# Three chained layers on one core: first-stage tiles shifted by 32 bytes, a bit step moved from GpSimd to VectorE, and stores, spools, weight loads and second-MLP inputs given other slots and places

## The chip, the cores and the metric

The kernel runs on one core of a Trainium2 chip. The metric is the device time of one execution in microseconds (us). The engines are TensorE (PE; its weight loads are PEld), VectorE (DVE), ScalarE (ACT), GpSimd (POOL) and SyncE (SP). Each works through its own queue in program order. SP issues every DMA of this kernel, so a DMA that must wait holds all DMAs behind it.

## The reference

```python
scores = scale * np.matmul(q_c, k_c.transpose(0, 1, 2, 4, 3))    # chunks of 64 positions
attn = softmax(scores); out = np.matmul(attn, v_c)               # 8 x 8 heads, 576 x 64 -> x: 4608 x 512
gate = 1.0 / (1.0 + np.exp(-(x @ w_gate)))                       # 512 x 1536
x = (gate * (x @ w_val)) @ w_out                                 # 1536 x 512
h = x @ w_in                                                     # 512 x 2048
g = np.where(h >= 1, h, np.where(h <= -1, 0.0, (h + 1) ** 2 / 4))
return g @ w_out2                                                # 2048 x 512
```

The activations arrive as float32, the weights as 64-bit floats, which the kernel must turn into float32 itself.

## The kernel before

**Precision.** Every large product is done as three fp32r matmuls of a high and a low part (`three`, L455 to L457). A weight tile goes through a chain of steps: `w_load` (DMA of the 64-bit words into a tile called raw), `w_low` (L114, a multiply and a min on the lower words), `w_bits` (L120 on DVE, L124 on ACT), `w_join` (L128, DVE), then the split into high (ACT) and low (POOL) parts.

**Stage 1** (0 to 795 us) goes over nine blocks of 512 rows. A block has 24 slots, and a slot is one projection: 12 matmuls of 512 columns, gate and value by turns. Between the projections of block b lies the chunk attention of block b+1 for four pairs of heads, by the methods of `Whole`: transpose, scores (S), maximum and subtraction on DVE, exponential on ACT, sum and reciprocal on DVE (L337 to L340), the scaling on POOL (`w`, L345, tile sp), a transpose of the result on PE (PT, L351), and the product with V (O). The gate times the value is formed on DVE (L854, tile sg) and stored to DRAM (gT).

What is issued in which slot is written by hand: `at(slot, prio, fn)` puts a call in a slot, and `emit(slot)` issues the calls ahead of the slot's projection, by the fraction of the slot and then by prio. Block 0 also converts 24 gate and value tiles, most of them one a slot. From slot 26 (block 1) to block 7 the weights of the later layers are prepared in 22 pairs, one in 7 slots, by the table `s_prep`: load, convert, four sums on POOL (L150 to L153), four splits (L172, L173) into tiles called st, and seven DMAs that store (spool) them to DRAM.

**Stages 2 to 4** are the three further products, each with one level of a seven-product block scheme (PO = 1, 5, 6, 2, 7, 3, 4): "o" (x @ w_out, `down`), "i" (h = x @ w_in, `up`) and "p" (g @ w_out2, `down`). Each goes over six groups of 768 rows, in steps of six matmuls of 384 columns (`on(step, prio, fn)` is the table of calls here). A group is 42 steps in "o" and 56 in "i" and "p". Operands are prepared some steps ahead: a subtraction (`op_sub`, L488), the high part (`op_hi`, ACT L492) and the low part (`op_lo`, L499, POOL or DVE). Results are gathered in tiles R; "o" stores them to yT, "i" stores its activations (tile ua) to uT. The weights of a stage come back from DRAM into 28 places of the pool wp (`s_load`, L187), while the stage before still runs.

**Places.** wp lies at the bottom of SBUF; its tiles of 4 KiB start 1,152 bytes above a multiple of 4 KiB. From the top downwards lie a pad of 128 bytes, a larger pad, then the tiles x of stage 1 (4 KiB each, 1,120 bytes above a multiple of 4 KiB), sg and raw. In "o" the operands (tile op) take the places of x.

Of the kernel before, what the change touches and what calls it, by code (L numbers as in the profile page):

```python
# [8 lines left out]
F32 = mybir.dt.float32  # L9
# [20 lines left out]
def kernel(  # L30
# [15 lines left out]
    nc = tc.nc  # L46
    P = 128
# [63 lines left out]

    def w_low(key):
        word = words(raws[key])
        nc.gpsimd.tensor_scalar(  # L114
            out=word(0, I32), in0=word(0, U32), scalar1=2.0**-29, scalar2=7.0, op0=ALU.mult, op1=ALU.min
        )

# [76 lines left out]
    def s_prep(kind, k):  # L194

        half_ = (F1 if kind == "o" else F2) // 2
        a, b = (kind, k), (kind, k + half_)
        return [
            (0, w_load, a), (0, w_load, b), (2, w_low, a), (2, w_low, b), (3, w_bits, a), (4, w_bits, b),
            (5, w_join, a), (5, w_join, b), (6, s_sums, kind, k), (7, s_split, kind, k, 0), (7, s_split, kind, k, 1),  # L200
            (8, s_split, kind, k, 2), (8, s_spool, kind, k, 0), (8, s_spool, kind, k, 1),
            (9, s_split, kind, k, 3), (9, s_spool, kind, k, 2), (10, s_spool, kind, k, 3),
        ]


# [170 lines left out]
    def first_block():  # L376
        ft = ps.tile([P, BS], F32, tag="b5", name="fill")

        def fill(n):
            for _ in range(n):  # L380
                nc.tensor.matmul(ft, lhsT=z[:, :P], rhs=z, start=True, stop=True)

        pieces = []
        for i in range(NW + 1):
            pieces.append((w_bits, keys[i]))
            pieces.append((w_low, keys[i + 1]))
            if i:
                pieces.append((w_split, keys[i - 1]))
        pieces.insert(0, (w_low, keys[0]))
        nl = [0]  # L390

        def wl(n):
            for _ in range(n):
                w_load(keys[nl[0]])
                nl[0] += 1

        def conv(n):
            while n and pieces:
                fn, key = pieces.pop(0)
                fn(key)  # L400
                if fn is w_split and nl[0] < NW + 5:
                    wl(1)
                n -= fn is not w_low
            if pieces and pieces[0][0] is w_low:
                w_low(pieces.pop(0)[1])

        z = pool["sg"].tile([P, BS], F32R, tag="sg", name="z", bufs=4)
        nc.vector.memset(f32(z), 0.0)
        kv_["ident"] = cp.tile([P, P], F32, name="ident")
        make_identity(nc, kv_["ident"])  # L410
        a = Whole(
            0, [["b0", "b2", "b4"], "b1", "b3", "b6", "b7", "b5"],
            lambda nm: wp.tile([P, 2, BS], F32, tag="w", name=nm), "MVMT",
        )
# [115 lines left out]
    def down(kind, nk, tile_, load0, load1, done, first=0):  # L530

        t0, half_ = len(steps), nk * 7
        for g in range(NG):
            for i, (p, k) in enumerate((p, k) for p in PO for k in range(nk)):
# [19 lines left out]
                for m in range(2):  # L554
                    if k == (nk // 2 - 1 if split and m == 0 else nk - 1):
                        dt = m if p != 4 else 0
                        on(t + 1 + dt, 1, down_result, g, p, m)
                        done(t + 1 + dt, g, m, p)

    def down_step(kind, g, p, ks, ms=(0, 1)):  # L560
        for k in ks if isinstance(ks, list) else [ks]:
            o = OP[kind, g, p, k]
            w = s_weight(kind, p, k)
            for m in ms:
                cols = slice(m * P, (m + 1) * P)
                product(p, m, [(k == 0, (w[:, 0, cols], w[:, 1, cols], o[:, 0], o[:, 1]))], g % 2)

    def down_result(g, p, m):
        if p == 1:
            R_[m] = pool["r"].tile([P, 4, N], F32, tag="R", name="R", bufs=3)  # L570
        r = R_[m]
        result(p, banks[BANK[p], m], lambda i: r[:, i])

# [27 lines left out]
    NY = 22  # L601

    def z_tile(i, dt=F32R):
        return pool["za" if i < 14 or i >= NY else "zb"].tile([P, 2, N], dt, tag=f"z{i}", name="z")

    def z_flat(i):
        return z_tile(i, F32).rearrange("p h t -> p (h t)")
# [21 lines left out]
    def up_result(p, m):  # L629
        b = banks[BANK[p], m]  # L630
        if p in (1, 5):
            shape = [P, 2, N] if p == 1 else [P, N]
            R_[p, m] = pool["r"].tile(shape, F32, tag=f"R{p}", name="R", bufs=3 if p == 1 else 4)
        if p == 4:
            nc.scalar.activation(U[1, m][:, 0], b, AF.Relu, scale=0.5, bias=half)
            R_["b", m] = b
        else:
            result(p, b, lambda i: R_[5, m] if i == 3 else R_[1, m][:, i])
# [108 lines left out]
    for i, key in enumerate(keys):  # L747
        if i >= NW + 5:
            at(i - NW - 5, 2.5, w_load, key)
        if i > NW + 1:  # L750
            at(i - NW - 2, 6, w_low, key)
        if i > NW:
            at(i - NW - 1, 6, w_bits, key)
        if i >= NW:
            at(i - NW, 5.5, w_split, key)
# [29 lines left out]
    for i in range(7):  # L785
        on(2 * 7 * F1 // 2 + 6 * i, 9, s_load, "i", i)
    for s in range(1, 7 * F1 // 2, 2):
        on(last + s, 9, s_load, "i", 7 + s // 2)
    on(tc_ - 6, 9, close_pool, "m3")
    on(tc_ - 6, 9.1, open_pool, "za", "za")  # L790
    for i in range(2):
        on(tc_ - 6, 9.2, y_in, 0, i)
    on(tc_, 2, close_pool, "r")
    on(tc_, 2, close_pool, "x")
    on(tc_, 2, close_pool, "pad4")
# [7 lines left out]
    td = len(steps)  # L803
    last = td - 14 * NJ
    for i in range(NWT["p"]):
        on(last + 2 * i + 4, 9, s_load, "p", i)
    for i in range(F2 // 2):
        on(last + 12 + 2 * i, 9, p_in, 0, 0, i)
        on(last + 30 + i if i < 4 else td + i - 4, 9, p_in, 1, 0, i)
# [16 lines left out]
    with tc.manual_schedule():  # L826
# [3 lines left out]
        nc.vector.memset(minus, -0.5)  # L830

        open_pool("pad", "pad", "right")
        pool["pad"].tile([P, 32], F32, name="pad")

        open_pool("pad4", "pad4", "right")
        pool["pad4"].tile([P, 704], F32, name="pad4")
# [8 lines left out]
        for b in range(NB):  # L845
            for f in range(F1):
                slot = NS * b + 2 * f
                emit(slot)
                go = proj(("g", f), b, f"b{f % 2}")
                sg = pool["sg"].tile([P, BS], F32, tag="sg", name="sg", bufs=4)  # L850
                nc.scalar.activation(sg, go, AF.Sigmoid)  # L851
                emit(slot + 1)
                vo = proj(("v", f), b, f"b{2 + f % 2}")
                nc.vector.tensor_tensor(out=sg, in0=vo, in1=sg, op=ALU.mult)  # L854
                nc.sync.dma_start(out=gT[b][f * P:(f + 1) * P, :], in_=sg)
        close_pool("sg")
        assert not ev, ev
        open_pool("r", "rb", "right")
# [2 lines left out]
            fn(*args)  # L861
        for t in sorted(sched):
            run_step(t)
        for key in ("r", "zb", "pad", "za"):
            close_pool(key)


# [28 lines left out]
```

## Time and profile before

| | |
|---|---|
| three timed runs | 1786.47, 1787.66, 1787.59 us (median 1787.59) |
| the profiled execution | 1787.38 us; its span 1785.6 us |
| PE busy | 1699.8 us, 95% |
| PEld, DVE, ACT, POOL busy | 86%, 64%, 48%, 56% |
| mean granted TensorE clock | 0.981 |
| DMA, read and written | 179.83 MB and 125.30 MB, 171 GB/s |

The span runs from the first to the last instruction. The granted clock is 1.0 at 2.4 GHz and 0.5 at 1.2 GHz. A busy PE is not PE at its peak, since matmuls are pipelined; how many matmuls of one kind a stretch holds says more than its busy time.

### The profile page before, as it was taken

The numbers are of one execution on the slowest core, as the hardware profiler recorded it, in microseconds if no ns is written. First come the engines' busy times: TensorE is split into PE (matmuls) and PEld (weight loads), VectorE is DVE, ScalarE is ACT, GpSimd is POOL, SyncE is SP. The second block draws the span as 40 slices with busy tenths as digits, with TensorE's granted clock in tenths as the row PEclk, the third lists the DMA queues.
The fourth block names the chain that finished last, engine by engine and source line by source line (L and its number), as shares of the span: only waits on it lengthen the run. The fifth ranks groups of instructions, "written<-read, shape, count | busy, mean of one in ns | idle before, by whom it ended". The sixth has DMA issues, their size and how long they took to land.

```text
span 1785.6 us, 29925 instructions
## 1 busy us (share of the span) xinstructions
PE 1699.8 (95%) x10658; PEld 1542.2 (86%) x10658; DVE 1147.0 (64%) x1659; ACT 864.8 (48%) x1560; POOL 993.6 (56%) x826
## 2 busy tenths in 40 slices
PE   6889999899899899999999989999999989999998
PEld 5667777677677677889999989999999989999998
DVE  4664444444444453129877757878887798889886
ACT  4553454444444454125555545555555445455553
POOL 4982554565554554017777755434442167777775
PEclk8899999999999999999999999999999999999999
DMA  8653666666666766754464573334235944644552
GB/s 202 164 135 98 195 193 178 197 209 196 201 173 196 210 198 192 247 195 135 152 221 142 161 264 116 142 142 156 111 142 200 412 152 111 173 145 104 133 151 36
DMA packets 389702, 307.15 MB, mean 172 GB/s; under 512 B 271920, under 2 KB 302640, under 8 KB 389552
## 3 DMA queue, kind: packets, MB, share of 16 engines
q1 hardware_dynamic: 389552, 305.23, 55.7%
q8 instruction: 84, 1.38, 0.3%
q14 instruction: 66, 0.54, 0.1%
HBM read 179.83 MB, written 125.30 MB: 171 GB/s over the span
## 4 chain that ended last, share of the span: by engine, by line
PE 72%; DMA 7%; SPq 7%; POOL 5%; DVE 4%; issue 3%; ACT 1%; DVEq 0%; POOLq 0%; ACTq 0%
PE P L456 16%; PE P L457 16%; PE P L455 16%; PE pr L455 8%; PE pr L457 7%; PE pr L456 7%; SPq L278 4%; POOL raw L114 2%; DMA z<-uT 1%; SPq L288 1%; DMA raw<-in_moe_w_out_dram 1%; PE O L361 1%; DMA uT<-ua 1%; DVE z L488 1%; DMA raw<-in_moe_w_gate_dram 1%
## 5 line engine op out<-in xcount | busy, mean ns | idle before, releaser
L499 POOL TENSOR_TENSOR z<-z 128x384 fp32r<-128x384 f32 x308 | 358.2, 1186 | 319.5 <-ACT z L492 252.9
L456 PE MATMUL P<-z,w 128*128 128x384 f32 x1344 | 452.8, 337 | 9.1 <-DVE z L499 5.4
L455 PE MATMUL P<-z,w 128*128 128x384 f32 x1344 | 452.0, 336 | 4.9 <-ACT z L492 3.5
L457 PE MATMUL P<-z,w 128*128 128x384 f32 x1344 | 451.4, 336 | 0.0
L455 PE MATMUL pr<-x,w 128*128 128x512 f32 x864 | 357.4, 414 | 0.0
L456 PE MATMUL pr<-x,w 128*128 128x512 f32 x864 | 346.7, 401 | 0.0
L457 PE MATMUL pr<-x,w 128*128 128x512 f32 x864 | 345.9, 400 | 0.0
L854 DVE TENSOR_TENSOR sg<-pr,sg 128x512 f32<-128x512 f32 x108 | 74.6, 691 | 343.2 <-PE pr L457 194.3
L492 ACT ACTIVATE z<-z 128x384 fp32r<-128x384 f32 x420 | 205.8, 521 | 183.4 <-DVE z L488 101.6
L499 POOL TENSOR_TENSOR op<-in,op 128x384 fp32r<-128x384 f32 x168 | 193.9, 1174 | 147.9 <-ACT op L492 147.1
L456 PEld LDWEIGHTS P<-z,w 128*128 128x128 f32 x1344 | 253.7, 189 | 12.2 <-DVE z L499 6.6
L455 PEld LDWEIGHTS P<-z,w 128*128 128x128 f32 x1344 | 253.7, 189 | 6.2 <-ACT z L492 4.4
L457 PEld LDWEIGHTS P<-z,w 128*128 128x128 f32 x1344 | 253.7, 189 | 0.0
L457 PEld LDWEIGHTS pr<-x,w 128*128 128x128 f32 x864 | 165.7, 192 | 40.6
L455 PEld LDWEIGHTS pr<-x,w 128*128 128x128 f32 x864 | 165.9, 192 | 40.1
L114 POOL TENSOR_SCALAR raw<-raw 128x512 int32<-128x512 uint32 x68 | 143.9, 2116 | 96.6 <-DMA raw<-in_moe_w_out_dram 50.1
L456 PEld LDWEIGHTS pr<-x,w 128*128 128x128 f32 x864 | 166.1, 192 | 35.6
L851 ACT ACTIVATE sg<-pr 128x512 f32<-128x512 f32 x108 | 64.3, 596 | 255.4 <-PE pr L457 253.8
L492 ACT ACTIVATE op<-in 128x384 fp32r<-128x384 f32 x252 | 128.2, 524 | 113.7 <-PE P L457 53.4
L488 DVE TENSOR_TENSOR z<-z 128x384 f32<-128x384 f32 x200 | 169.7, 899 | 8.5 <-POOL z L499 8.5
L456 PE MATMUL P<-op,w 128*128 128x384 f32 x504 | 169.5, 336 | 0.3 <-DVE op L499 0.3
L457 PE MATMUL P<-op,w 128*128 128x384 f32 x504 | 169.4, 336 | 0.0
(63 smaller groups left out, 2406.8 us busy)
## 6 DMA issues: line engine op xcount, KB each, us to landing
uT<-ua SPq DMA_DIRECT2D x96, 384.0 KB, 2.3
z<-uT SPq DMA_DIRECT2D x96, 384.0 KB, 3.8
gT<-sg SPq DMA_DIRECT2D x108, 256.0 KB, 2.7
in<-gT SPq DMA_DIRECT2D x72, 256.0 KB, 4.0
raw<-in_moe_w_out_dram SPq DMA_DIRECT2D x28, 512.0 KB, 4.8
swi<-st SPq DMA_DIRECT2D x56, 256.0 KB, 4.2
swp<-st SPq DMA_DIRECT2D x56, 256.0 KB, 3.0
w<-swi SPq DMA_DIRECT2D x28, 512.0 KB, 4.6
```

The costliest lines, as they stand in the source:

```text
L114: nc.gpsimd.tensor_scalar(out=word(0, I32), in0=word(0, U32), scalar1=2.0**-29, scalar2=7.0, op0=ALU.mult, op1=ALU.min)
L278: nc.sync.dma_start(out=t[32 * g:32 * g + 32, i, off // 32:(off + m) // 32], in_=rows[h, :, 32 * j:32 * j + 32].rearrange("(t i) r -> i t ...
L288: nc.sync.dma_start(out=t[hs, off // CH:(off + m) // CH], in_=v[bb, 2 * p + h, s0:s0 + m].rearrange("(c k) d -> k c d", k=CH),)
L361: nc.tensor.matmul(banks[h][hs, ts], lhsT=self.V[p][hs, c], rhs=self.SP[p][hs, 1, ts], start=True, stop=True)
L455: nc.tensor.matmul(o, lhsT=ah, rhs=bh, start=first, stop=False, skip_group_check=open_)
L456: nc.tensor.matmul(o, lhsT=ah, rhs=bl, start=False, stop=False, skip_group_check=open_)
L457: nc.tensor.matmul(o, lhsT=al, rhs=bh, start=False, stop=last, skip_group_check=open_)
L488: (eng or nc.vector).tensor_tensor(out=op_src(p, key), in0=x, in1=y, op=ALU.subtract)
L492: nc.scalar.activation(o[:, 0], op_src(p, key), AF.Copy)
L499: eng.tensor_tensor(out=o[:, 1], in0=op_src(p, key), in1=f32(o[:, 0]), op=ALU.subtract)
L851: nc.scalar.activation(sg, go, AF.Sigmoid)
L854: nc.vector.tensor_tensor(out=sg, in0=vo, in1=sg, op=ALU.mult)
```

## The change

1. `w_low` runs on DVE (`nc.vector`) and no longer on POOL, for all 68 tiles; in the first block and for the gate and value tiles it stands directly ahead of its `w_bits`.
2. `s_prep` spreads a pair: conversion four and five slots after the load (it was two to four), sums at seven, splits at eight to ten, spools at ten to twelve.
3. The store of sg to gT is issued at the start of the next even slot, and no longer right behind the product.
4. R has two tiles in "o" (three before, three still in "p"); in "i" the tile R1 has four (three before).
5. The four input tiles of "i" (y_in) have a pool "y" of their own, which opens as stage 1 ends; the first of them are loaded 20 steps ahead of "i" and no longer 6.
6. The loads of "i" weights come one in three steps (before: one in two) and go on into "i"; those of "p" come three in ten steps (one in two) and go on into "p".
7. The pad is 96 bytes, so that x, sg, raw, op and R move up by 32 bytes; x then starts 1,152 bytes above a multiple of 4 KiB, as the weights do.

```diff
 def w_low(key):
-        nc.gpsimd.tensor_scalar(
+        nc.vector.tensor_scalar(
             out=word(0, I32), in0=word(0, U32), scalar1=2.0**-29, scalar2=7.0, op0=ALU.mult, op1=ALU.min
...
-            (0, w_load, a), (0, w_load, b), (2, w_low, a), (2, w_low, b), (3, w_bits, a), (4, w_bits, b),
-            (5, w_join, a), (5, w_join, b), (6, s_sums, kind, k), (7, s_split, kind, k, 0), (7, s_split, kind, k, 1),
-            (8, s_split, kind, k, 2), (8, s_spool, kind, k, 0), (8, s_spool, kind, k, 1),
-            (9, s_split, kind, k, 3), (9, s_spool, kind, k, 2), (10, s_spool, kind, k, 3),
+            (0, w_load, a), (0, w_load, b), (4, w_low, a), (4, w_bits, a), (5, w_low, b), (5, w_bits, b),
+            (6, w_join, a), (6, w_join, b), (7, s_sums, kind, k), (8, s_split, kind, k, 0), (8, s_split, kind, k, 1),
+            (9, s_split, kind, k, 2), (10, s_spool, kind, k, 0), (10, s_spool, kind, k, 1),
+            (10, s_split, kind, k, 3), (11, s_spool, kind, k, 2), (12, s_spool, kind, k, 3),
...
-            R_[m] = pool["r"].tile([P, 4, N], F32, tag="R", name="R", bufs=3)
+            R_[m] = pool["r"].tile([P, 4, N], F32, tag="R", name="R", bufs=2 + (steps_kind[0] == "p"))
...
-        return pool["za" if i < 14 or i >= NY else "zb"].tile([P, 2, N], dt, tag=f"z{i}", name="z")
+        return pool["za" if i < 14 else "y" if i >= NY else "zb"].tile([P, 2, N], dt, tag=f"z{i}", name="z")
...
-            R_[p, m] = pool["r"].tile(shape, F32, tag=f"R{p}", name="R", bufs=3 if p == 1 else 4)
+            R_[p, m] = pool["r"].tile(shape, F32, tag=f"R{p}", name="R", bufs=4)
...
-        if i > NW + 1:
-            at(i - NW - 2, 6, w_low, key)
         if i > NW:
+            at(i - NW - 1, 6, w_low, key)
             at(i - NW - 1, 6, w_bits, key)
...
-        on(last + s, 9, s_load, "i", 7 + s // 2)
+        on(last + 3 * s // 2, 9, s_load, "i", 7 + s // 2)
...
-        on(tc_ - 6, 9.2, y_in, 0, i)
+        on(tc_ - 20, 9.2, y_in, 0, i)
...
-        on(last + 2 * i + 4, 9, s_load, "p", i)
+        on(last + 4 + 10 * i // 3, 9, s_load, "p", i)
...
-        pool["pad"].tile([P, 32], F32, name="pad")
+        pool["pad"].tile([P, 24], F32, name="pad")
...
-                nc.sync.dma_start(out=gT[b][f * P:(f + 1) * P, :], in_=sg)
+                at(slot + 2, 7, g_store, b, f, sg)
```

On POOL, in block 0, the scaling of the attention (L345) stood between conversions of weight tiles (L114 is `w_low`, L138 the low part of a tile). Before:

```order
L345 TENSOR_TENSOR sp<-sp,r 128x512
L138 TENSOR_TENSOR w<-raw,w 128x512
L114 TENSOR_SCALAR raw<-raw 128x512
L138 TENSOR_TENSOR w<-raw,w 128x512
L114 TENSOR_SCALAR raw<-raw 128x512
```

The same stretch of POOL's queue now:

```order
L345 TENSOR_TENSOR sp<-sp,r 128x512
L138 TENSOR_TENSOR w<-raw,w 128x512 x5
L345 TENSOR_TENSOR sp<-sp,r 128x512
L138 TENSOR_TENSOR w<-raw,w 128x512 x5
L345 TENSOR_TENSOR sp<-sp,r 128x512
```

A whole step of the conversion has left POOL; only L138 and L345 are in its queue. On DVE, at the second attention of the same block (L120 and L128 convert, L337 to L340 form the sum and its reciprocal for L345), before:

```order
L854 TENSOR_TENSOR sg<-pr,sg 128x512
L128 SCALAR_TENSOR_TENSOR raw<-raw 128x512
L120 SCALAR_TENSOR_TENSOR raw<-raw 128x512
L337 TENSOR_REDUCE l<-sp 128x8
L338 TENSOR_SCALAR l<-l 128x8
L340 RECIPROCAL r<-l 128x8
L128 SCALAR_TENSOR_TENSOR raw<-raw 128x512
L120 SCALAR_TENSOR_TENSOR raw<-raw 128x512
```

And now:

```order
L857 TENSOR_TENSOR sg<-pr,sg 128x512
L128 SCALAR_TENSOR_TENSOR raw<-raw 128x512
L114 TENSOR_SCALAR raw<-raw 128x512
L120 SCALAR_TENSOR_TENSOR raw<-raw 128x512
L337 TENSOR_REDUCE l<-sp 128x8
L338 TENSOR_SCALAR l<-l 128x8
L340 RECIPROCAL r<-l 128x8
L128 SCALAR_TENSOR_TENSOR raw<-raw 128x512
L114 TENSOR_SCALAR raw<-raw 128x512
L120 SCALAR_TENSOR_TENSOR raw<-raw 128x512
```

DVE has one instruction more for each tile, ahead of L120, and the order of the rest is as it was; in the stretch of the pairs too L114 and L120 stand ahead of L337 for some pairs. On SP, ahead of the loads of the sixth pair (in block 2; L855 and L741 are the store to gT, L278 and L288 the loads of q, k and v). Before:

```order
L855 DMA gT_68<-sg 128x512 x2
L278 DMA qk<-in_q_dram 32x8x32 x8
L278 DMA qk<-in_k_dram 32x8x32 x8
L288 DMA vd<-in_v_dram 64x3x64
L288 DMA vd<-in_v_dram 64x5x64
L288 DMA vd<-in_v_dram 64x3x64
L288 DMA vd<-in_v_dram 64x5x64
L109 DMA raw<-in_moe_w_out_dram 128x512 x2
L855 DMA gT_68<-sg 128x512
```

And now:

```order
L183 DMA swo_88<-st 128x512
L278 DMA qk<-in_q_dram 32x8x32 x8
L278 DMA qk<-in_k_dram 32x8x32 x8
L741 DMA gT_68<-sg 128x512
L288 DMA vd<-in_v_dram 64x3x64
L288 DMA vd<-in_v_dram 64x5x64
L288 DMA vd<-in_v_dram 64x3x64
L288 DMA vd<-in_v_dram 64x5x64
L109 DMA raw<-in_moe_w_out_dram 128x512 x2
L741 DMA gT_68<-sg 128x512
```

The loads of q and k, and so those of the pair, stand behind one store fewer. On SP around the first step of "i" (L612 is y_in, L595 the last store of R in "o", L187 the weight loads), before:

```order
L187 DMA w<-swi_132 128x1024
L612 DMA z<-yT_75 128x768 x4
L187 DMA w<-swi_133 128x1024
L187 DMA w<-swi_134 128x1024
L187 DMA w<-swi_135 128x1024
L595 DMA yT_80<-R 128x2x768 x2
L612 DMA z<-yT_76 128x768 x4
L656 DMA uT_81<-ua 128x768 x12
```

And now:

```order
L187 DMA w<-swi_122 128x1024
L612 DMA z<-yT_75 128x768 x4
L187 DMA w<-swi_123 128x1024
L187 DMA w<-swi_124 128x1024
L187 DMA w<-swi_125 128x1024
L187 DMA w<-swi_126 128x1024
L187 DMA w<-swi_127 128x1024
L187 DMA w<-swi_128 128x1024
L595 DMA yT_80<-R 128x2x768 x2
L612 DMA z<-yT_76 128x768 x4
L187 DMA w<-swi_129 128x1024
L187 DMA w<-swi_130 128x1024
```

The first y_in (yT_75) has moved ahead of ten weight loads, and the last store of "o" and the second y_in (yT_76) ahead of seven.

## Rows read from the trace of the kernel before

**Rows 1.** The page: busy time of each engine and share of the span.
```profile
PE 1699.8 (95%) x10658; PEld 1542.2 (86%) x10658; DVE 1147.0 (64%) x1659; ACT 864.8 (48%) x1560; POOL 993.6 (56%) x826
```

**Rows 2.** Windows of stage 1 (start, blocks 0-6, 8): length, busy PE PEld DVE ACT POOL, clock, DMA.
```profile
0.00:41.88 41.88, 24.53 (x346) 20.99 (x346) 20.26 (x46) 20.04 (x28) 18.09 (x17) 0.82 0.85 201
41.88:143.95 102.07, 85.58 (x593) 66.49 (x593) 64.59 (x107) 57.82 (x84) 84.32 (x46) 0.92 0.57 145
143.95:230.50 86.55, 80.84 (x562) 63.53 (x561) 36.68 (x68) 36.08 (x53) 36.78 (x31) 0.96 0.56 158
230.50:311.30 80.80, 77.62 (x563) 61.33 (x562) 36.54 (x68) 36.95 (x55) 42.65 (x37) 1.00 0.63 183
311.30:396.95 85.65, 79.31 (x561) 62.48 (x560) 40.91 (x72) 38.58 (x58) 48.70 (x42) 0.96 0.68 205
396.95:484.50 87.55, 79.70 (x561) 62.71 (x560) 38.55 (x68) 37.68 (x57) 46.86 (x39) 0.96 0.66 192
484.50:562.20 77.70, 77.43 (x561) 61.22 (x560) 39.40 (x72) 37.60 (x56) 42.72 (x37) 1.00 0.69 201
562.20:650.85 88.65, 80.50 (x561) 63.06 (x561) 39.24 (x69) 38.55 (x58) 47.14 (x41) 0.96 0.63 185
...
727.25:794.50 67.25, 67.25 (x289) 54.12 (x289) 8.77 (x13) 9.87 (x18) 4.03 (x4) 1.00 0.71 250
```

**Rows 3.** Waits of PE: line waited for, us in total, times, longest.
```profile
PE PT L351 <- POOL sp L345: 50.8, 18, 5.6
```

**Rows 4.** Groups by line in block 0: busy us, mean ns, idle before.
```profile
L114 POOL TENSOR_SCALAR raw<-raw 128x512 int32<-128x512 uint32 x19 | 41.6, 2188 | 1.6
...
L128 DVE SCALAR_TENSOR_TENSOR raw<-raw 128x512 int32<-128x512 int32 x21 | 18.1, 862 | 3.4 <-ACT raw L124 3.0
L120 DVE SCALAR_TENSOR_TENSOR raw<-raw 128x512 int32<-128x512 int32 x20 | 15.5, 776 | 25.1 <-POOL raw L114 25.1
```

**Rows 5.** Timeline of a stall in block 2: start us, us, instruction, idle before.
```profile
282.76 1.08 SPq L109 DMA_DIRECT2D raw<-in_moe_w_out_dram  x2
...
287.52 4.54 POOL L114 TENSOR_SCALAR raw<-raw 128x512 int32<-128x512 uint32 x2 [10.24 <-DMA raw<-in_moe_w_out_dram]
...
289.53 0.69 DVE L120 SCALAR_TENSOR_TENSOR raw<-raw 128x512 int32<-128x512 int32 x1 [5.65 <-POOL raw L114]
...
294.67 0.66 PE L351 MATMUL PT<-ident,sp 128*128 128x128 f32 x4 [3.18 <-POOL sp L345]
```

**Rows 6.** Timeline of the start: the first attention's way to PE.
```profile
16.68 0.69 DVE L120 SCALAR_TENSOR_TENSOR raw<-raw 128x512 int32<-128x512 int32 x1 [3.97 <-POOL raw L114]
...
18.12 2.00 POOL L114 TENSOR_SCALAR raw<-raw 128x512 int32<-128x512 uint32 x1 [1.48 <-DMA raw<-in_moe_w_gate_dram]
...
20.20 1.59 POOL L345 TENSOR_TENSOR sp<-sp,r 128x512 f32<-128x512 f32 x1
```

**Rows 7.** Timelines of SP, ACT and PE where "i" begins.
```profile
1059.35 0.89 SPq L595 DMA_DIRECT2D yT<-R  x2
...
1066.69 0.49 ACT L514 ACTIVATE R<-P 128x384 f32<-128x384 f32 x1 [4.36 <-DMA yT<-R]
...
1081.75 0.44 PE L456 MATMUL P<-z,w 128*128 128x384 f32 x1 [1.18 <-POOL z L499]
```

**Rows 8.** Windows within "o", around "i"'s start, within "i", around "p"'s start.
```profile
880.00:920.00 40.00, 40.00 (x233) 40.00 (x232) 32.26 (x41) 22.52 (x47) 29.80 (x27) 1.00 0.70 240
1050.00:1090.00 40.00, 33.60 (x166) 31.08 (x165) 17.93 (x25) 17.19 (x37) 19.55 (x19) 0.91 0.53 199
1120.00:1160.00 40.00, 40.00 (x232) 40.00 (x232) 32.20 (x44) 22.02 (x41) 16.10 (x14) 1.00 0.37 138
1400.00:1440.00 40.00, 34.89 (x191) 34.26 (x190) 31.58 (x43) 18.57 (x36) 13.18 (x11) 0.96 0.96 385
1440.00:1480.00 40.00, 37.57 (x212) 36.41 (x211) 34.57 (x43) 21.15 (x46) 30.12 (x26) 1.00 0.32 96
```

**Rows 9.** Waits of ACT for the activations' stores, 1395 to 1475 us.
```profile
ACT ua L643 <- DMA uT<-ua: 9.9, 7, 5.6
```

More of the change, by code (lines that the diff above doesn't have):

```diff
@@ L384, in first_block @@
         for i in range(NW + 1):
+            pieces.append((w_low, keys[i]))
             pieces.append((w_bits, keys[i]))
-            pieces.append((w_low, keys[i + 1]))
             if i:
                 pieces.append((w_split, keys[i - 1]))
-        pieces.insert(0, (w_low, keys[0]))
         nl = [0]
@@ L403, in conv @@
                 n -= fn is not w_low
-            if pieces and pieces[0][0] is w_low:
-                w_low(pieces.pop(0)[1])
         z = pool["sg"].tile([P, BS], F32R, tag="sg", name="z", bufs=4)
@@ L558, in down @@
                         done(t + 1 + dt, g, m, p)
+    steps_kind = [None]
     def down_step(kind, g, p, ks, ms=(0, 1)):
+        steps_kind[0] = kind
         for k in ks if isinstance(ks, list) else [ks]:
@@ L738, in emit, with g_store @@
             fn(*args)
+    def g_store(b, f, sg):
+        nc.sync.dma_start(out=gT[b][f * P:(f + 1) * P, :], in_=sg)
     later_block(1, [5 * p for p in range(KT)], (0, 1, 1.5, 2, 3, 3, 5, 5.5, 7, 7.5, 8))
@@ L764 @@
     at(base, 8, close_pool, "raw")
+    at(base, 8.1, open_pool, "y", "y")
     at(base, 8.1, open_pool, "m3", "m3")
@@ L854 @@
                 nc.vector.tensor_tensor(out=sg, in0=vo, in1=sg, op=ALU.mult)
-                nc.sync.dma_start(out=gT[b][f * P:(f + 1) * P, :], in_=sg)
+                at(slot + 2, 7, g_store, b, f, sg)
+        emit(NS * NB)
         close_pool("sg")
@@ L863 @@
             run_step(t)
-        for key in ("r", "zb", "pad", "za"):
+        for key in ("r", "zb", "pad", "za", "y"):
             close_pool(key)
```

## The prediction

> **What bounds the kernel now.** The page's busy times come first: PE 95%, DVE 64%, POOL 56% [rows 1]. A PE that is 95% busy leaves little, unless its work is slowed, so next I read windows, one for each block of stage 1 [rows 2]. Seven blocks do the same matmuls and last 77.70 to 102.07 us. Block 5 shows no fall of the clock and 77.43 of 77.70 us busy: that is the floor of a block with attention. Block 0 lies 24.4 us above it, blocks 1 to 4 and 6 lie 8.85, 3.1, 7.95, 9.85 and 10.95 above, 40.7 in sum. A long block has a granted clock of 0.92 or 0.96: stretches at the lower level lengthen "busy" time, so the busy share hides part of what a wait costs. The waits of PE name one line: PT waits for POOL's scaling sp, 18 times, 50.8 us [rows 3].
>
> The timeline of one such stall shows the chain [rows 5]. SP issues the pair's loads at 282.76, behind q, k, v and a store of gT. POOL's L114 waits 10.24 us for the load and then does two tiles in 4.54; DVE's L120 waits 5.65 for POOL; the row sum, which stands behind L120 on DVE, and the scaling, which stands behind L114 on POOL, are late; PE waits 3.18. So a weight tile that nobody needs soon stops attention twice, on POOL and on DVE. In block 0 the same chain is permanent: POOL is busy 84.32 of 102.07 us (83%), L114 takes 41.6 of them, and DVE's L120 stands idle 25.1 us for L114 [rows 2, 4].
>
> Between the stages the windows show too few matmuls: 166 where 232 or 233 fit into 40 us [rows 8]. A matmul of 384 columns is thus 40/232.5 = 0.172 us, and the start of "i" lacks 66.5 of them, 11.4 us; around "p" 41 and 20 are lacking, 10.5 us.
>
> The sum is made against the profiled execution, 1787.38 us (span 1785.6 and 1.8 around it), which is 0.2 below the median of the runs.
>
> **w_low on DVE, start.** The first sp runs at 20.20 on POOL, directly behind an L114 of 2.00 us that ends at 20.12, and L120 ahead of it waited 3.97 [rows 6]. Without L114 the scaling could start up to 2 us earlier, and the sum up to 3.97 earlier less 0.69 for L114 on DVE. I take −3; bounds 0 (the load alone sets it) and −6 (both in full).
>
> **w_low on DVE, block 0.** POOL falls to 84.3 − 41.6 = 42.7 us and is no bound. DVE gets 19 instructions. The trace shows no L114 on DVE; the nearest row is L120, same engine, words and shape, with one operand more: 0.69 us where POOL is quiet [rows 5, 6], 0.776 in the mean of block 0 [rows 4]. I take 0.69: 19 × 0.69 = 13.1. As POOL's L114 goes, I let L120 and L128 fall to 0.69 too, an estimate: 20 × 0.086 + 21 × 0.172 = 5.3. DVE then has 64.6 + 13.1 − 5.3 = 72.4 us. If it fills 83% of the block, as POOL did as the bound, the block takes 87.5 us: −14. Bounds: L114 at nothing gives 59.3/0.83 = 71, under the floor, so −24; L114 at POOL's 2.19 gives 64.6 + 41.6 − 5.3 = 101, over 0.83 = 122, so +20.
>
> The Trainium skill, "VectorE: DVE Perf Modes", section "The perf-mode tier table", speaks for the better end: a tensor_scalar on fp32 in SBUF runs at twice the rate of two-operand forms (1227 against 2293 ns for 2048 elements). By it L114 would take about 0.42 us (an estimate), DVE 67 us, the block 81, and the term −21. No row here shows that form on these words.
>
> **Blocks 1 to 6, w_low and the spread of s_prep.** Three things leave the path at once. L114 no longer stands ahead of the scaling on POOL: two of them were 4.54 us in the stall, more than PE's 3.18 [rows 5]. No step on POOL lies between the landing and DVE's L120. And DVE first touches a raw tile in slot four; before, POOL touched it in slot two and DVE in slot three. A slot is 77.70/24 = 3.2 us. The stall's L114 waited for a landing; DVE touches the tile 3.2 us later than before, and had waited 5.65 us for it, of which 2.0 to 4.5 were POOL's own step. What is left as a wait, 5.65 − 3.2 − 2.3 = 0.2 us, the slack of attention can hide. Added on DVE are 44 × 0.69 = 30 us in six blocks, 5 each, on an engine at 37 to 41 of 80 us. I leave 5 of the 40.7: −36. Bounds: −41 (all), and −28 if L114 at the two slots costs its own wait in a third of the stalls.
>
> The spools two slots later hold raw and st tiles longer. The next pair comes seven slots after, a raw tile is read last by the splits in slot ten, and POOL's and DMA's part is the same in number. Cost 0, hidden by the slots in which a tile stood unused.
>
> **The store of sg later** takes one store out of the way of the q, k and pair loads on SP. sg has several tiles; one comes per two slots, 6.5 us. 0 by itself; its gain is within the −36.
>
> **"o" to "i".** Of the 11.4 us part is a wait of ACT's L514 for the last stores of R (4.36 us, issued 1059.35) and part PE's wait for the low part z, 1.18 at 1081.75 [rows 7]. y_in no longer waits for places: loaded 20 steps ahead, it is out of that jam. But the tiles R of "i" still lie where those of "o" lay, so the wait for the store of yT remains, and the second y_in still needs that store's data. I take −2; bounds −7 (all but the 4.36) and +2 (R with two tiles in "o": a store must land before the tile is refilled).
>
> **R with two tiles in "o"**, between its groups: a store in stage 3 to 4 cost ACT 9.9/7 = 1.4 us in the mean, 5.6 at worst [rows 9]; the refill comes some 5 us after the store is issued, and operands are prepared steps ahead. 0; bound +8 (five boundaries at 1.4, and a little clock).
>
> **"i" to "p".** Loads of 28 tiles of 0.52 MB in 56 steps (6 × 0.172 = 1.03 us each) ask for 14.7 MB in 58 us, 253 GB/s, beside 138 of the stage's own [rows 8]: 391, and the row shows 385 at a busy share of 0.96, DMA full. ACT's waits for the stores of uT, 9.9 us, are its sign [rows 9]. In 94 steps the loads ask for 151, together 289 GB/s, 0.72 of the share. Then the 7.0 us of 1400 to 1440 mostly go; the 3.5 after 1440, the start of a stage without its results, stay. I take −5; bounds 0 and −9. A tile that comes later must still be ahead of its use: the table leaves 16 steps or more, 16 us, so 0 for that.
>
> **The 32 bytes.** Matmuls of 512 columns take 67.25/288 = 233.5 ns in block 8 [rows 2]. In "o" the operand has x's place, in "i" another, and both give 232 or 233 matmuls in 40 us [rows 8]. So the offset made no difference there, and I take 0.
>
> Sum: −3 − 14 − 36 − 2 − 5 = −60; 1787.4 − 60 = 1727.4, say **1727.5**.
>
> **The rivals.**
>
> *DVE takes POOL's place.* In block 0 DVE goes from 64.6 to over 72 us with the sum and reciprocal in the same queue; a conversion that waits there for a load or for ACT's L124 (L128 already waits 3.0 [rows 4]) stops attention as POOL did. Then block 0 keeps its 102 (+14) and a third of the stall cost of blocks 1 to 6 stays (+9, beyond the 5): 1750. For it: two steps in one queue without a slot between. Against it: DVE was idle 25.1 us for POOL alone.
>
> *The places do matter.* x moves to the weights' offset, and PE reads both in each matmul. A matmul of 384 columns takes 172 ns against 160 for its columns alone at 2.4 GHz, 12 to 13 more; one of 512 takes 233.5 against 213.3, 20 more. If 512 came down to the same 13, it would be 226.7: 9 × 24 × 12 = 2592 matmuls × 6.8 ns = −17.6, so 1710. Against it: [rows 8] as above.
>
> The Trainium skill, "TensorE: Matmul & The Clock Gate", section "Back-to-back issue gap", gives N/2.4 + 2.5 ns, 216 ns at 512 columns. No stretch here reaches that; by it the case would be worth 2592 × 17.5 ns = 45 us, 1682.
>
> *All goes to the floor.* Block 0 reaches 77.7 (a further −10), the start of "i" and blocks 1 to 6 are clean (−9): 1708. For it: DVE was at only 64.6 us, and ACT 57.8 and POOL 42.7 are below the floor.
>
> *The other side: late loads stop DVE.* DVE now is the first to touch a raw tile. A load that has not landed in slot four stops subtraction, sum and gate, not only the scaling. The waits of 50.8 us stand beside 65.1 us of excess, so a waited microsecond costs 1.3. It decides from (40.7 + 14 + 3 + 7)/22 = 2.9 us a pair; at the longest wait seen, 5.6, a pair costs 7.2, 22 pairs 158, the kernel 1787 + 158 − 65 = 1880. Against it: 3.2 us more between load and touch.
>
> **How the numbers follow.** Forecast 0.58, own range 1715 to 1743; DVE in POOL's place 0.18 at 1750; places 0.09 at 1710; floor 0.09 at 1708; late loads 0.06, half of them with a cost near 2.9 us a pair and no change, half beyond. 0.2%, 3.6 us, is about what a measurement of this kernel can tell. Faster 0.94, same 0.03, slower 0.03. The range 1706 to 1756 holds forecast, floor, places and DVE's case, and leaves their far ends and the late loads out, 0.2 in all.
>
> **What the profile after would show.** L114 on DVE, 68 times, at about 0.69 us (0.42 by the perf mode); PE's wait for sp down from 50.8 to under 10 us; block 0 near 88, blocks 1 to 6 at 77.7 to 79.5 with a clock of 1.0; the wait of L514 for yT still there, that of L643 for uT gone; 288 matmuls of 512 columns still in 67.25 us. The prediction is wrong if DVE's L114 shows several microseconds of idle time for the DMA of raw with a late sp behind it, if block 0 stays near 100 with DVE over 80%, or if the spacing of the 512-column matmuls has changed.

## The result, and the profile after

The changed kernel takes 1716.13 us (median of four runs, 1715.86 to 1721.92), the kernel before 1787.03 beside it: a ratio of 0.9612 [0.9591, 0.9633] (95% interval), 71 us or 3.9% less. The forecast was 1727.5, with a range of 1706 to 1756.

The page after, busy times, to be read beside [rows 1]:

```profile
PE 1669.7 (97%) x10658; PEld 1530.4 (89%) x10658; DVE 1168.1 (68%) x1727; ACT 866.6 (51%) x1560; POOL 836.3 (49%) x758
```

DVE has 68 instructions more and POOL 68 fewer. PE does the same 10658 matmuls in 30 us less busy time: it ran less at the lower clock (0.990 granted in the mean, 0.981 before), and the windows show a second reason. Windows of stage 1 after (columns as in [rows 2]):

```profile
0.00:40.55 40.55, 23.88 (x347) 20.16 (x347) 21.38 (x50) 18.82 (x26) 7.83 (x12) 0.79 0.81 202
40.55:130.95 90.40, 81.28 (x594) 64.03 (x594) 74.80 (x129) 58.74 (x85) 36.59 (x27) 0.96 0.64 166
130.95:206.85 75.90, 75.90 (x562) 61.29 (x561) 38.27 (x74) 34.91 (x52) 21.60 (x24) 1.00 0.62 169
206.85:282.70 75.85, 75.85 (x561) 61.26 (x560) 39.25 (x74) 38.05 (x57) 32.73 (x33) 1.00 0.71 201
282.70:358.60 75.90, 75.90 (x561) 61.27 (x560) 41.59 (x80) 38.22 (x56) 26.50 (x29) 1.00 0.72 209
358.60:436.00 77.40, 76.06 (x562) 61.28 (x560) 40.58 (x75) 38.65 (x57) 32.73 (x36) 1.00 0.72 212
436.00:512.55 76.55, 75.95 (x561) 61.28 (x560) 41.00 (x78) 37.78 (x56) 28.54 (x31) 1.00 0.75 213
512.55:594.65 82.10, 78.28 (x561) 63.04 (x560) 39.71 (x77) 39.01 (x58) 31.55 (x34) 0.96 0.79 226
...
669.70:735.00 65.30, 65.30 (x290) 54.07 (x289) 8.77 (x13) 9.88 (x18) 4.02 (x4) 1.00 0.72 258
```

Blocks 1 to 3 lie at 75.9 us, under the 77.70 that the prediction took for the floor. Block 8, all projections, went from 67.25 to 65.3 us: 226.7 ns a matmul and no longer 233.5. The waits of PE after, first to 131 us, then from there to 735, and last one of the kernel before in its block 0:

```profile
PE S L315 <- DVE qkT L298: 7.9, 4, 3.1
...
PE PT L351 <- POOL sp L345: 5.0, 2, 4.3
```

```profile
PE S L315 <- DVE qkT L298: 5.1, 2, 3.8
```

```profile
PE S L315 <- DVE qkT L298: 3.8, 3, 1.9
```

The line that cost 50.8 us [rows 3] is down to 5.0, and 4.3 of them lie in the start. PE's wait for DVE's transposes of q and k (L298) grew from 3.8 to 13.0. Groups by line after, block 0 (columns as in [rows 4]), then L114 in blocks 1 to 6:

```profile
L120 DVE SCALAR_TENSOR_TENSOR raw<-raw 128x512 int32<-128x512 int32 x21 | 17.7, 842 | 0.7
L128 DVE SCALAR_TENSOR_TENSOR raw<-raw 128x512 int32<-128x512 int32 x22 | 17.0, 771 | 3.6 <-ACT raw L124 3.4
...
L114 DVE TENSOR_SCALAR raw<-raw 128x512 int32<-128x512 uint32 x20 | 11.0, 550 | 1.2 <-DMA raw<-in_moe_w_gate_dram 1.2
```

```profile
L114 DVE TENSOR_SCALAR raw<-raw 128x512 int32<-128x512 uint32 x40 | 16.6, 416 | 33.1 <-DMA raw<-in_moe_w_in_dram 16.9 <-DMA raw<-in_moe_w_out_dram 16.2
```

Windows around the start of "i" and of "p" after, beside [rows 8] (the first of "p" begins 11 us ahead of its first matmul, that of [rows 8] 20):

```profile
990.00:1030.00 40.00, 37.08 (x207) 35.39 (x207) 24.47 (x34) 19.88 (x41) 25.59 (x23) 1.00 0.54 196
...
1340.00:1380.00 40.00, 38.23 (x211) 37.76 (x210) 34.42 (x47) 20.49 (x44) 20.04 (x18) 0.96 0.75 278
1380.00:1420.00 40.00, 37.54 (x214) 36.59 (x213) 31.96 (x42) 20.04 (x43) 31.09 (x27) 1.00 0.70 222
```

207 matmuls stand where 166 did at the start of "i". From the first matmul of a part to the first of the next, in us, before and after: start 41.9 and 40.5; block 0 102.1 and 90.4; blocks 1 to 6 506.9 and 463.7; blocks 7 and 8 143.6 and 140.3; "o" 262.7 and 262.5; first group of "i" 69.7 and 62.7, the rest 293.6 and 291.2; first group of "p" 67.3 and 65.3, the rest to the last matmul 291.2 and 292.0. The differences make -70.4 of the -71.1 between the spans.

### The profile page after: what moved, and what is told of

It reads as the page before. It is cut to its first block, busy times and chain, and to the rows that moved or that the text cites. A ratio compares the mean times of both kernels' runs of the same rounds, so it can differ in the third digit from the quotient of the medians.

```text
span 1714.5 us, 29990 instructions
## 1 busy us (share of the span) xinstructions
PE 1669.7 (97%) x10658; PEld 1530.4 (89%) x10658; DVE 1168.1 (68%) x1727; ACT 866.6 (51%) x1560; POOL 836.3 (49%) x758
## 4 chain that ended last, share of the span: by engine, by line
PE 85%; DVE 5%; SPq 4%; DMA 3%; issue 1%; ACT 1%; POOL 1%; DVEq 0%; ACTq 0%; POOLq 0%
PE P L453 17%; PE P L454 17%; PE P L452 17%; PE pr L452 10%; PE pr L454 10%; PE pr L453 10%; SPq L278 3%; PE O L361 2%; DVE z L485 1%; DMA raw<-in_moe_w_val_dram 1%; PE S L315 1%; SPq L288 1%; PE PT L351 1%; DVE z L496 1%; POOL z L496 0%
## 5 line engine op out<-in xcount | busy, mean ns | idle before, releaser
L452 PE MATMUL pr<-x,w 128*128 128x512 f32 x864 | 349.1, 404 | 0.2 <-ACT x L369 0.2
L454 PE MATMUL pr<-x,w 128*128 128x512 f32 x864 | 339.4, 393 | 0.0
L453 PE MATMUL pr<-x,w 128*128 128x512 f32 x864 | 338.9, 392 | 0.3 <-DVE x L374 0.3
L452 PEld LDWEIGHTS pr<-x,w 128*128 128x128 f32 x864 | 163.3, 189 | 36.2 <-ACT x L369 0.6
L454 PEld LDWEIGHTS pr<-x,w 128*128 128x128 f32 x864 | 163.4, 189 | 35.5
L453 PEld LDWEIGHTS pr<-x,w 128*128 128x128 f32 x864 | 163.8, 190 | 32.3 <-DVE x L374 0.6
L453 PE MATMUL P<-op,w 128*128 128x384 f32 x504 | 168.5, 334 | 0.1
L454 PE MATMUL P<-op,w 128*128 128x384 f32 x504 | 168.4, 334 | 0.0
L452 PE MATMUL P<-op,w 128*128 128x384 f32 x504 | 168.4, 334 | 0.0
L513 DVE TENSOR_TENSOR R<-P,R 128x384 f32<-128x384 f32 x216 | 116.1, 552 | 76.2 <-PE P L454 69.8
```

Source lines behind the costliest of these rows:

```text
L452: nc.tensor.matmul(o, lhsT=ah, rhs=bh, start=first, stop=False, skip_group_check=open_)
L453: nc.tensor.matmul(o, lhsT=ah, rhs=bl, start=False, stop=False, skip_group_check=open_)
L454: nc.tensor.matmul(o, lhsT=al, rhs=bh, start=False, stop=last, skip_group_check=open_)
L513: nc.vector.tensor_tensor(out=r(i), in0=b, in1=r(i), op=ALU.add)
```

## The experiments

Twelve kernels ran, on four chips; each ratio is to the kernel before, run beside it on the same chip (its medians there: 1793.1 for x1 to x4, 1791.0 for x5 to x8, 1793.3 for x9 to x11 and 1790.3 us for x12). The table has, from one trace of each kernel, by first matmuls as above, in us: block 0; the excess of blocks 1 to 6 over six times their floor (77.3 us where a 512-column matmul takes 233 ns, 75.9 where it takes 227, 76.2 at 229); block 8; the first group of "i"; the last group of "i" and the first of "p".

| kernel | ratio | block 0 | excess 1-6 | block 8 | "i" first | last "i", first "p" |
|---|---|---|---|---|---|---|
| before | 1 | 102.1 | 43.1 | 67.2 | 69.7 | 60.1, 67.3 |
| changed | 0.9612 [0.9591, 0.9633] | 90.4 | 8.3 | 65.3 | 62.7 | 58.2, 65.3 |
| x1: changed, pad 128 | 0.9614 [0.9584, 0.9645] | 92.5 | 0 | 67.2 | 64.2 | 58.4, 66.9 |
| x2: before, pad 96 | 0.9941 [0.9921, 0.996] | 104.1 | 44.9 | 65.3 | 69.1 | 60.0, 67.4 |
| x3: before, w_low on DVE | 0.9875 [0.9853, 0.9898] | 97.9 | 29.2 | 67.2 | 69.1 | 59.5, 67.3 |
| x4: changed, w_low on POOL | 1.0006 [0.9988, 1.0024] | 159.1 | 10.6 | 65.3 | 62.8 | 58.2, 65.3 |
| x5: changed, old s_prep | 0.9722 [0.9688, 0.9756] | 92.5 | 30.3 | 65.3 | 64.4 | 58.2, 65.3 |
| x6: changed, sg stored at once | 0.9597 [0.9576, 0.9618] | 95.5 | 5.3 | 65.3 | 62.6 | 58.2, 65.3 |
| x7: changed, again | 0.9599 [0.9566, 0.9632] | 92.8 | 8.3 | 65.3 | 63.1 | 58.2, 65.3 |
| x8: y_in at 6, old loads of "p" | 0.9618 [0.9599, 0.9638] | 93.5 | 8.1 | 65.3 | 64.2 | 59.8, 67.3 |
| x9: x at 1,216, old loads of "i" | one run, 1720.8 | 89.9 | 5.1 | 65.9 | 69.3 | 58.3, 65.4 |
| x10: x at 1,184, no pool y | one run, 1727.5 | 94.6 | 0 | 67.2 | 65.0 | 58.3, 65.4 |
| x11: later steps, earlier L298 | 0.9579 [0.9552, 0.9606] | 96.3 | 3.6 | 65.3 | 64.5 | 58.2, 65.3 |
| x12: later steps, w_low twice | 0.963 [0.9606, 0.9654] | 103.8 | 5.7 | 65.3 | 64.4 | 58.2, 65.3 |

Single traces differ where nothing was edited. Block 0 takes 89.9 to 94.6 us in the changed kernel and in x1, x5, x7, x8, x9 and x10, whose edits do not touch it beyond the pad, and the first group of "i" 62.6 to 64.5 in the changed kernel and in x1, x4, x5, x6, x7, x11 and x12, whose edits do not touch it beyond the pad. Smaller differences in these two columns say nothing.

### The places: x1, x2, x9, x10

x1, in the changed kernel (x2 is the same edit the other way in the kernel before; in x9 the pad is 8 and in x10 16 elements):

```diff
-        pool["pad"].tile([P, 24], F32, name="pad")
+        pool["pad"].tile([P, 32], F32, name="pad")
```

x9 also has `on(last + s, 9, s_load, "i", 7 + s // 2)`; x10 also has y_in's tiles in the pool "za" at 6 steps, R with three tiles in "o" and R1 with three.

> The changed kernel with the pad at 128 bytes again, so that x starts at 1,120 and not at 1,152 bytes above a multiple of 4 KiB. If the place sets the time of a 512-column matmul: block 8 goes from 65.2 us back to 67.2, every block of stage 1 is about 2 us longer, matmuls are 233.5 ns apart and not 226.7, and the kernel is 2592 x 6.8 ns = 17 us slower, 1731 to 1734. If the faster matmuls come from something else in the change (fewer collisions with DMA or with GpSimd): the pad changes nothing, 1716, and the spacing stays at 226.7 ns.

> The kernel before with the pad alone changed to 96 bytes. Places as cause: spacing 226.7 ns, block 5 at 75.8 us, block 8 at 65.2. The blocks that wait keep part of it for the waits, so between -9 and -17 us: 1770 to 1778, 1772 as the likeliest. If x's place does nothing: 1787.

> The changed kernel with two edits that act at different places. The pad is 32 bytes, so that x starts at 1,216 bytes above a multiple of 4 KiB, which is 64 bytes from the weights' 1,152 and like it a multiple of 64 (1,120 is not). If a multiple of 64 is what counts: spacing 226.7 ns, block 8 at 65.3 us. If x must have the weights' own offset: 233.3 ns, 67.2 us. And the loads of i weights come one in two steps as before: if these loads, ahead of the last store of yT on SP, were most of the 7 us at the start of i, its first group goes from 63 us to 67 or more; if not, it stays within 62 to 64.5.

> The changed kernel with two edits that act at different places. The pad is 64 bytes, x at 1,184 above a multiple of 4 KiB, a multiple of 32 and not of 64. If a multiple of 64 counts or the weights' own offset: 233.3 ns and block 8 at 67.2 us. If any offset at or above the weights' does: 226.7 ns and 65.3. And the tiles of y_in are in their old pool, loaded 6 steps ahead, with R of o in three tiles and R1 of i in three as before: if the places of y_in were the gain at the start of i, its first group goes from 63 us to 67 or more; y_in's time alone cost 1 us in an earlier run, so without an effect of the places it stays under 65.

Windows of x1, block 6 and block 8:

```profile
515.15:592.40 77.25, 77.25 (x562) 61.31 (x561) 39.64 (x77) 38.69 (x58) 31.42 (x33) 1.00 0.79 232
...
668.85:736.05 67.20, 67.20 (x289) 54.11 (x289) 8.76 (x13) 9.87 (x18) 4.00 (x4) 1.00 0.70 250
```

The pad alone sets the spacing of these matmuls, whose moving operand is x and whose stationary one is the weight. Over the 288 matmuls of block 8 it is 233.3 ns with x at 1,120, 226.7 at 1,152, 233.3 at 1,184 and 228.9 at 1,216: the two multiples of 64 bytes are fast, the two of 32 alone slow, and the weights' own offset is not needed for most of it. x9 thus fell between its two expected values, and why 1,216 lies 2.2 ns above 1,152 stays open. The weights never moved, so a start of x on 64 bytes and a distance of 64 bytes from the weights' start are not told apart. (sg and raw move with x, but the projections read only x and the weights, which stay.)

The size was missed. I expected x1 17 us slower; its ratio is that of the changed kernel, and the interval of x7, on another chip, overlaps too. The reason stands in the column of excess: x1 and x10, slow matmuls, have none, while the changed kernel has 8.3 twice. Six blocks take 463.5 us in x1 and 463.7 in the changed kernel. The faster matmuls gave 1.4 us a block and, in blocks 4 to 6, waits took it back. x2 is 10.6 us faster than the kernel before (0.59% of 1793.1; 9 to 17 were expected), and its block 0, where POOL sets the length, did not get shorter at all. What the places surely give is 1.4 us of block 7 and 1.9 of block 8.

### w_low, the spread and the store: x3 to x6

x3, in the kernel before (x4 is the reverse in the changed one; x5 takes the old table of s_prep, x6 calls g_store at once, both in the changed kernel):

```diff
-        nc.gpsimd.tensor_scalar(
+        nc.vector.tensor_scalar(
```

> The kernel before with w_low on DVE and nothing else. If L114 ahead of the scaling on POOL was what made PE wait: block 0 falls from 102 to about 92, blocks 1 to 6 lose more than 20 of their 40.7 us of excess, 1787 - 33 = 1754 (1745 to 1762). If the landing of the pair's load at two slots was what set it: blocks 1 to 6 keep 25 us or more of excess, since DVE now waits itself for the load two slots after it, and only block 0 and the start gain: 1770 to 1780, or above 1787 when DVE's wait also stops the maximum and the sum.

> The changed kernel with w_low back on POOL, in the places of the new order. If POOL's work ahead of the scaling was the cause: block 0 is back at 100 us or more (+11) and blocks 1 to 6 have 10 to 25 us of excess again: 1740 to 1755. If the later slots of the spread alone took the stalls away: only block 0 is slower, 1725 to 1730.

> The changed kernel with the table s_prep of before: w_low on DVE, but two slots behind the load. Theory now: in blocks 1 to 6 the later slots did most, since the run with w_low on DVE alone kept 29 us of excess and the run with w_low on POOL in the new slots kept 11. Then blocks 1 to 6 have 18 to 30 us of excess, and the kernel is 12 to 25 us slower than the changed one beside it. Rival, the store of sg: the loads now stand behind one store fewer on SP and land early enough for the old slots; then excess stays under 10 us and the kernel within 5 us of the changed one.

> The changed kernel with the store of sg issued right behind the product, as before. If the spread of s_prep is the cause: excess of blocks 1 to 6 stays at 0 to 8 us, the kernel within 4 us of the changed one. If the store in front of the loads on SP is: 10 to 25 us of excess and as much slower. Block 0 tells it too: 90 to 92 us without an effect, 95 or more with one.

> The changed kernel itself, beside the others on one chip. Spacing of 512-column matmuls 226.7 ns, block 8 at 65.0 us, blocks without a wait at 75.9; 1716 to 1722. The waits in blocks 4 to 6 of its first profile (8 us of excess) may be there or not: a run with the pad alone put back had none.

The table is nearly a two-by-two for blocks 1 to 6: neither edit 43.1 us of excess, w_low on DVE alone 29.2, the new slots alone 10.6 (x4), both 8.3. With the pad at 96 bytes in all four, the corners are 44.9 (x2), 30.3 (x5), 10.6 and 8.3; x4 and x5 keep the other edits of the change. The later slots are worth 22 to 34 us, w_low on DVE 14 without them and 2 with them, which is less than such traces differ by (5.1 to 8.3 in the changed kernel, x6, x7, x8 and x9). x3 came out by its second branch, the landing of the load: 1770.9 us and more than 25 of excess. The store of sg did nothing that can be seen in the time or the excess: x6 and x7 have ratios of 0.9597 and 0.9599. A block 0 of 95 us or more was to be the sign of an effect, and x6 has 95.5; but x10, with the store moved, has 94.6. Why the old slots fail with w_low on DVE shows in x5's waits of DVE (us in total, times, longest), blocks 1 to 6:

```profile
DVE raw L114 <- DMA raw<-in_moe_w_out_dram: 58.0, 19, 14.2
...
DVE raw L114 <- DMA raw<-in_moe_w_in_dram: 35.2, 14, 12.2
```

DVE stands 93.2 us for loads that have not landed, against 33.1 in the changed kernel (the group of L114 above). Behind them sp is late again: PE waits 23.3 us for it in x5's blocks 1 to 6. That is the mechanism of the rival "late loads stop DVE", kept small only by the two slots.

x4 missed by 40 us, all of it in block 0: 159.05 us. Its waits there:

```profile
DVE raw L120 <- POOL raw L114: 87.7, 21, 5.4
...
PE PT L351 <- POOL sp L345: 35.1, 4, 8.9
PE S L315 <- DVE qkT L298: 25.8, 4, 8.2
```

In the new order w_low stands directly ahead of its w_bits. On one engine that costs nothing; across two, DVE waits 4.2 us for each tile, and DVE's other work (L298) with it. So x4 does not price POOL's load; it shows that the order and the engine belong together.

### The starts of "i" and "p": x8, x9, x10

x8, in the changed kernel:

```diff
-        on(tc_ - 20, 9.2, y_in, 0, i)
+        on(tc_ - 6, 9.2, y_in, 0, i)
...
-        on(last + 4 + 10 * i // 3, 9, s_load, "p", i)
+        on(last + 2 * i + 4, 9, s_load, "p", i)
```

> The changed kernel with two things put back that act at different places: y_in is issued 6 steps ahead of i (in its own places still), and the loads of p weights come one in two steps. If y_in's early load gave the 7 us at the start of i: its first group goes from 62.7 back to 66 to 70 us. If it was the fewer weight loads ahead of the store of yT: the first group stays at 62 to 64. For p, if full DMA was the cause: the last group of i goes from 58.2 to 60 us and the first of p from 65.3 to 67.3, 3.8 together; if the loads are hidden anyway: no change there. Together +4 to +10 us on the changed kernel.

With y_in late the first group of "i" takes 64.2 us, which is within the spread of kernels that left it early; without its pool (x10) it takes 65.0, hardly beyond it and between the two expected values. With the old loads of "i" weights (x9) it is back at 69.3. ACT's waits there, x9 and then the changed kernel:

```profile
ACT R L511 <- DMA yT<-R: 6.5, 2, 5.5
```

```profile
ACT R L511 <- DMA yT<-R: 2.6, 2, 1.5
```

It is the store of yT behind the weight loads that lands late. It is issued at nearly the same moment, 0.6 us after the first matmul of "i" in x9 and 0.2 in the changed kernel, but takes 7.7 us in the mean to land and not 4.1. The second half landed 9.4 us after that matmul in the kernel before, 9.5 in x9 and 5.6 in the changed kernel and x8. x8's time is 4.4 us above x7's, but their intervals overlap, so its trace decides: the old loads of "p" bring back 3.6 us (1.6 in the last group of "i", 2.0 in the first of "p") and this wait, 1296 to 1416 us in x8:

```profile
ACT ua L643 <- DMA uT<-ua: 9.4, 6, 5.5
```

### What holds block 0, and a version meant to beat both: x11, x12

x11: L298 of block 1 one slot earlier, and all of s_prep from w_low on one slot later. x12: only the later steps of s_prep, and in block 0 a second w_low for each tile:

```diff
-    later_block(1, [5 * p for p in range(KT)], (0, 1, 1.5, 2, 3, 3, 5, 5.5, 7, 7.5, 8))
+    later_block(1, [5 * p for p in range(KT)], (-1, 1, 1.5, 2, 3, 3, 5, 5.5, 7, 7.5, 8))
...
             at(i - NW - 1, 6, w_low, key)
+            at(i - NW - 1, 6, w_low, key)
```

> A version meant to beat both. First, in block 0 the transposes of q and k on DVE (L298) are issued one slot earlier, ahead of the conversions that stand in front of them there. If DVE's queue is what delays S (PE waited 7.8 us for L298, and ran at the lower clock behind it): block 0 goes from 91 to 93 down to 82 to 87 us. If q and k land too late for that, or DVE is full anyway: 90 or more. Second, s_prep's steps behind the load are one slot later still. DVE's L114 waits for the landing of some loads in blocks 4 to 6, up to 8.9 us: if that wait is what is left of the excess, it falls from 8 us to 0 to 3. Both: 1703 to 1709 against 1716 to 1719.

> The changed kernel with s_prep one slot later, as in the run before, but with the transposes of block 0 in their old slots; and in block 0 each weight tile that is converted between the projections gets w_low twice (the second pass takes the last three bits of these weights away). That adds some 19 x 0.42 to 0.55 = 8 to 10 us to DVE in block 0 and nothing to another engine. If block 0 is set by how full DVE is (83% busy at 90 us): it goes from 90 to 93 us to 100 to 105. If it is set by the loads of q, k and raw on SP, or by the chain over ACT: 90 to 95. Blocks 1 to 6: 0 to 5 us of excess, where the changed kernel had 8 twice.

x11 failed in block 0: 96.3 us where 82 to 87 were hoped for. PE's wait for L298 fell from 7.9 to 2.4, and a wait of 6.6 for ACT's copy of the transposed result (L354, ahead of O) took its place. The later steps left 3.6 and 5.7 us of excess, little better than 8.3 and no better than x6 and x9, and x11's interval lies across the changed kernel's. x12's block 0 answers in part what holds it (window, then two groups of lines, 38 to 140 us):

```profile
38.30:142.10 103.80, 87.69 (x594) 68.91 (x594) 90.30 (x146) 57.91 (x84) 35.56 (x27) 0.89 0.56 145
```

```profile
L120 DVE SCALAR_TENSOR_TENSOR raw<-raw 128x512 int32<-128x512 int32 x20 | 25.0, 1250 | 0.7
L114 DVE TENSOR_SCALAR raw<-raw 128x512 int32<-128x512 uint32 x39 | 21.1, 540 | 0.7
```

DVE's work grew by 15.5 us (74.8 to 90.3) and the block by 13.4 against the changed kernel's first profile, 11.0 against its second. ACT and POOL did no more than before. So added work on DVE lengthens block 0 nearly one for one. That DVE's work alone sets it is not shown: with 73.6 to 76.2 us of that work the block took 89.9 to 97.9 us in ten kernels (the changed one, x1, x3 and x5 to x11). What makes up the rest stays open.

## Why the prediction was right, point by point

**The bound and the sum.** That PE was slowed by late sp and by a lower clock behind it, and that this would go, was right: -60 forecast, -71 measured. The 11 us beyond the forecast come from three places: blocks 1 to 6, the start of "i", and the faster matmuls of blocks 7 and 8, which stood in no term.

**Start, -3.** -1.4 between the two profiles, and PE's wait for sp there fell from 7.8 to 4.3. But over the kernels here the start lies between 36.7 and 43.7 us, 43.7 in the one with w_low alone moved. The term can't be told from this spread.

**Block 0, -14: right in kind, too large.** It measured -11.7, and -9.3 in x7. L114 cost 11.0 us, not 13.1, but the relief of 5.3 for L120 and L128 failed: 842 and 771 ns, where 0.69 was taken. That DVE then filled 83% of the block (74.80 of 90.40) as taken is luck: the share is 76% in x3, 80% in x7 and 87% in x12. w_low alone moved gives 4.2 us (x3, 97.9), no more than single traces differ by; what the new order of these steps adds no run tried apart. The Trainium skill, "VectorE: DVE Perf Modes", section "The perf-mode tier table", has tensor_scalar on fp32 in SBUF at twice the basic rate; the prediction's estimate from it, 0.42 us for L114, agrees with the 416 ns of blocks 1 to 6. The 550 ns of block 0, where single ones beside POOL's work last 1.27 us, show what the -21 left out.

**Blocks 1 to 6, -36: right in size, its parts not weighed.** The excess over the floor of the same pad fell by 34.8. 5 us of excess were forecast, 8.3 came. In all these blocks lost 43.2, as the floor fell by 8.4; with the old pad (x1) the excess is 0, so there the other edits alone take away the whole 43. That the forecast's 5 came near the 8.3 is partly luck. The prediction named three reasons as one; the runs rank them: the two slots first, w_low second.

**"o" to "i", -2: wrong by 5.** The step that failed is "the tiles R of "i" still lie where those of "o" lay, so the wait for the store of yT remains". The wait remained, but shrank from 4.4 to 2.6 us, since it is set by when the store lands, and that by the weight loads ahead of it on SP: -7.0 (-5.2 to -7.1 over the kernels with the new loads, x8 and x10 aside), of which x9 gives back 6.6. I had counted y_in's move and not the seven loads that moved with it, though the order showed them.

**"i" to "p", -5.** -3.8 measured, 3.6 by x8 alone: right. ACT's wait for the stores of uT is gone, as forecast.

**The 32 bytes, 0: the step was wrong, and cost little.** From two offsets that agree at 384 columns I inferred that none matters at 512. The spacing fell to 226.7 ns, to the tenth what the rival had worked out, which is luck as far as the 228.9 at 1,216 tells; its price of -17.6 was not met, since part of it is given back. A changed spacing was one of the prediction's own signs of being wrong, and for this step it was. The 216 ns that the Trainium skill gives for an isolated matmul ("TensorE: Matmul & The Clock Gate", "Back-to-back issue gap") were not reached at any of four offsets.

**The rival "late loads".** Its mechanism came, at 33.1 us of DVE's waits and 8.3 of excess. What was late behind L114 was S, by L298, and not sp as the sign had it. Such waits cost only where nothing covers them: x10 has 25.3 us of them and no excess, x1 11.4 and none. The timeline of the changed kernel's longest:

```profile
524.75 4.09 SPq L278 DMA_DIRECT2D qk<-in_q_dram  x8
528.88 5.16 SPq L278 DMA_DIRECT2D qk<-in_k_dram  x8
534.08 0.89 SPq L109 DMA_DIRECT2D raw<-in_moe_w_out_dram  x2
...
538.30 0.43 DVE L114 TENSOR_SCALAR raw<-raw 128x512 int32<-128x512 uint32 x1 [8.79 <-DMA raw<-in_moe_w_out_dram]
...
541.45 1.13 PE L315 MATMUL S<-qkT 64*64 64x64 f32 x32 [3.82 <-DVE qkT L298]
```

SP issues without a pause; 16 loads of q and k take 9.3 us ahead of the pair's. That a fuller SP is why faster matmuls bring waits back is argued from this stretch and the column of excess, not tried by itself.

**Two readings without weight.** The seven blocks do not hold quite the same matmuls: block 0 has 593 against 561 to 563 [rows 2], scores of one more pair of heads. And of the 44 tiles counted in six blocks 40 lie there, 16.6 us on DVE and not 30.

## What to carry to other kernels

A step that waits for a load should stand as many slots behind it as the issuing queue can be late: here, in blocks 1 to 6, two slots were worth more than the choice of engine. Two steps of one chain may stand side by side in one engine's queue, not in two engines' queues. When a stage waits for a store to land, count the loads issued ahead of that store, and when PE gets faster, look at which queue falls behind next (this last is argued, not shown).

## What the runs showed that was not expected

**A start on a multiple of 64 bytes.** With its moving operand on a multiple of 32 bytes only, a 512-column matmul took 233 ns, 4 to 7 more than on one of 64 (four offsets). At 384 columns there was next to nothing: the middle groups of "i" take 58.24 us in the changed kernel and 58.39 in x1, those of "o" 43.68 in both.

**DVE and POOL take turns.** Timeline of the changed kernel in block 0:

```profile
96.83 1.27 DVE L114 TENSOR_SCALAR raw<-raw 128x512 int32<-128x512 uint32 x1
98.13 1.69 DVE L120 SCALAR_TENSOR_TENSOR raw<-raw 128x512 int32<-128x512 int32 x1
...
101.23 0.42 DVE L114 TENSOR_SCALAR raw<-raw 128x512 int32<-128x512 uint32 x1
```

```profile
96.53 1.29 POOL L345 TENSOR_TENSOR sp<-sp,r 128x512 f32<-128x512 f32 x1 [2.36 <-PE pr L454]
97.78 1.50 POOL L138 TENSOR_TENSOR w<-raw,w 128x512 fp32r<-128x512 f32 x1
```

L114 begins while POOL's L345 runs (to 97.82) and ends at 98.10; L120 begins while L138 runs (to 99.28) and ends at 99.82. Each lasts 0.8 to 1.0 us longer than alone (0.42, 0.69). The Trainium skill, "SBUF — State Buffer", section "Who interferes with whom", says that a DVE instruction with two SBUF inputs contends with a GpSimd instruction that reads SBUF, and that one in a two-port mode and a GpSimd instruction block each other for a whole instruction. These rows agree, and x12's L120, 1250 ns in the mean, is the dearest case. So moving work from POOL to DVE does not keep POOL's remaining work out of DVE's way.
